# Split first up products, residual plus bias from PSUM, and a split last group in a spectral block with a squared-ReLU feed-forward

## The chip, the cores and the metric

The kernel runs on one core of one Trainium2 chip. The metric is device time in microseconds (us), the median of several executions. One execution was also taken by the hardware profiler; all times inside the kernel come from that one and count from the start of its span.

The engines are called as the profile calls them: PE is the matrix engine and PEld its weight load, DVE the vector engine, ACT the scalar engine, POOL the general engine (idle in the part treated here), SP the engine that issues DMAs. PSUM is the memory with eight banks into which PE writes its products.

## The reference

```python
def _A_ref(x, w_r, w_i):                       # spectral filter
    X = rfft2(x.astype(float32), axes=(-2, -1))
    X = X * (w_r + 1j * w_i)
    return irfft2(X, s=(2048, 512), axes=(-2, -1)).astype(bfloat16)

def _B_ref(x, w1, b1, w2, b2):                 # feed-forward, squared ReLU
    h = einsum("bsd,df->bsf", x, w1) + b1
    r = where(h > 0, h, 0)
    return einsum("bsf,fd->bsd", r * r, w2) + b2

x  = A_x                                       # 1 x 2048 x 512, bf16
h  = x + _A_ref(_layernorm(x), A_w_r, A_w_i)
h2 = h + _B_ref(_layernorm(h), B_w1, B_b1, B_w2, B_b2)   # F = 1792
```

The input `B_x` is not used. The layer norms have no weights of their own.

## The kernel before

The 2048 rows are laid out as 128 partitions by 16 row groups, g = 0 to 15, so that one group is a tile of 128 rows by 512 columns. The kernel has a spectral part, in which the transforms are matrix products with sine tables, and a feed-forward part. The change is in the feed-forward part and in the last inverse transform that feeds it.

**The order of the work.** Every operation is a task of a planner (`Plan`): an engine or a choice of engines, an assumed duration, what it reads and writes, a priority `prio` (small is early) and, for a buffer, an `alloc` tag with a limited number of copies. The planner simulates the engines with the assumed durations, picks at each step the task that can start first (the smallest `prio` among those that can start within 0.08 us of it), and emits the instructions in that order. Each engine then runs its list strictly in order, so an instruction that waits holds up all that stand behind it on its engine. `order` is a weaker form of `reads`: the task comes behind the named one if both are on one engine, and not before the start of the named one otherwise. `uses` keeps a buffer until the task has run.

**PSUM in this part.** Tag `ph` is one bank, `sg` two, `pp` three, `po` two. When a bank is taken and the planner sees PE without work for over 0.4 us ahead of it, `bank` (L678 to L682) first writes some dummy products into that bank (L681, up to 20), which keep PE from standing still. They wait for the bank like any other product.

**Chunks.** The feed-forward goes over five chunks of groups: `CHUNKS = ((0, 2), (2, 5), (5, 9), (9, 13), (13, 16))`. For chunk c the steps are:

- Inverse transform, last step. Chunk 0: `d5` (L703) gives even and odd halves, two groups times two halves; ACT and DVE copy them to `EO` (L708); `d6` adds in one `sg` bank `py` per group the identity product with x (k = 0, L788) and two transform steps (k = 1 and 2, L790 to L793), so that `py` holds h. Later chunks: `s5` (L726 to L729) into a `pp` bank, `od` (L734, ACT) copies its odd half, `lv1` (L739, two on DVE) forms sums and differences, and then one of two ways: groups in `BY_PE2` go straight to PE, `s6` with eight narrow products and one more (L756, L757); the others get a butterfly on DVE, `spec` (L764) and four `lv2` (L772), and then one wide product (L749). DVE adds x (L777, `hs`).
- Layer norm. Sum of squares on ACT (L665; for group 1 statistics on DVE, L803 and L805), a square root on ACT (L806, L840), a reciprocal and a product on DVE, then the normalised rows `u` (L817, L819; later chunks L851, L853).
- Transposes on PE (L828 for chunk 0, L872 for chunks 1 and 2; by DMA for chunks 3 and 4) and the copies to `UT` (L834, L880).
- In chunk 0, `hs` is copied out of `py` for both groups (L822, ACT or DVE). For every group `hb` = `hs` + b2 is formed on DVE (L780), in float32.
- Up products: 14 column blocks f (`NF`), each four products with the chunk's rows as moving operand (L894), into banks taken in turn from `ph`, `sg`, `sg`; then ReLU with bias on ACT (`relu`, L900) and the square on DVE (`sqr`, L906). One block reads all the rows of `UT`, so it waits for the copies of every group of the chunk.
- Down products: per group 14 products of 512 columns into a `po` bank (L915); DVE adds `hb` (`out_`, L923); SP sends the group to memory (L925).

The tasks of the next chunk's inverse transform and layer norm are placed among the up and down products of the chunk before; `early` and `late` are the priorities that do this.

Of the kernel before, what the change touches and what calls it, by code (L numbers as in the profile page):

```python
# [9 lines left out]
ALU = mybir.AluOpType  # L10
ACT = mybir.ActivationFunctionType
FP32 = mybir.dt.float32
BF16 = mybir.dt.bfloat16
# [127 lines left out]
def kernel(  # L141
# [567 lines left out]
            add(("ACT", "DVE"), (0.37, 0.36), deo, reads=[("pd", g, e)], order=[("EO", g, 1)] * (1 - e),  # L709
                writes=[("EO", g, e)], prio=z + g)  # L710

    BY_PE2 = (2, 3, 4, 5, 6)
    ONE = (1, 2, 3, 4)
    TURN = (3, 4)

    for c, (a, b) in enumerate(CHUNKS):
        n = b - a
# [2 lines left out]
        for g in range(a, b):  # L720
            z = late + g
            if c > 0:
                def s5(g=g):
                    p = bank(("p5", g), "pp", 3)
                    lh = [flat(T2[:, lt, g]) for lt in range(4)]
                    mm(p[:, 257:384], lhsT=lh[3], rhs=GI[:, 3, 127:0:-1], start=True, stop=True)  # L726
                    mm(p[:, 384:512], lhsT=lh[2], rhs=GI[:, 2, 128:0:-1], start=True, stop=True)
                    mm(p[:, 0:129], lhsT=lh[1], rhs=GI[:, 1, 128::-1], start=True, stop=True)
                    mm(p[:, 129:257], lhsT=lh[0], rhs=GI[:, 0, 127::-1], start=True, stop=True)  # L729
                add("PE", 0.26, s5, reads=["T2", "GI"], order=gate(c, g - a, n), writes=[("p5", g)], prio=early + 5, alloc=("pp", ("p5", g)))  # L730

                def od(g=g):
                    o = buf(ffn, ("od", g), "od", [P, 2, P], FP32, 2)
                    sc.copy(flat(o[:]), T["p5", g][:, 256:512])  # L734
                act(0.37, od, z, reads=[("p5", g)], order=[("sd", 0, 1)] * (c == 1), writes=[("od", g)], alloc=("od", ("od", g)))

                def lv1(g=g, i=0):
                    q = buf(ffn, ("q", g), "qb" if g in BY_PE2 else "q", [P, 2, 2, P], BF16 if g in BY_PE2 else FP32, 2) if i == 0 else T["q", g]
                    ve.tensor_tensor(q[:, i], T["p5", g][:, 0:256].rearrange("p (a c) -> p a c", a=2),  # L739
                                     T["od", g][:, ::-1, :], (ALU.add, ALU.subtract)[i])  # L740
                for i in range(2):
                    dve(0.36, lambda g=g, i=i: lv1(g, i), z, reads=[("p5", g), ("od", g)],
                        order=[("qh", g)] * i + [("n2", 0, 1)] * (c == 1),
                        writes=[("q", g), ("qh", g)] if i == 0 else [("q", g)], alloc=("qb" if g in BY_PE2 else "q", ("q", g)) if i == 0 else None)

                def s6(g=g):
                    p = bank(("p6", g), "pp", 3)
                    if g not in BY_PE2:
                        mm(p[:], lhsT=KI[:, 0], rhs=T["R", g][:], start=True, stop=True)  # L749
                        return  # L750
                    q = T["q", g]
                    for k in range(4):
                        o = p[:, 128 * k + 1:128 * k + 128]
                        for b in range(2):
                            v = q[:, k // 2, b, :0:-1] if k % 2 == 0 else q[:, k // 2, b, 1:]
                            mm(o, lhsT=KI[:, 1 if b == 1 and k in (1, 2) else 0], rhs=v, start=(k == 0 and b == 0), stop=False)  # L756
                    mm(p[:].rearrange("p (a b c) -> p a b c", a=2, b=2)[:, :, ::-1, 0], lhsT=KI[:, 0], rhs=q[:, :, :, 0],  # L757
                       start=False, stop=True)
                if g in BY_PE2:
                    add("PE", 0.5, s6, reads=[("q", g)], writes=[("p6", g)], prio=early + 4, alloc=("pp", ("p6", g)))  # L760
                else:
                    def spec(e, g=g):
                        R = buf(ffn, ("R", g), "R", [P, 512], BF16, 3)
                        COPY[e](R[:].rearrange("p (a b c) -> p a b c", a=2, b=2)[:, :, ::-1, 0], T["q", g][:, :, :, 0])  # L764
                    add(("DVE", "ACT"), (0.2, 0.27), spec, reads=[("q", g)], writes=[("R", g), ("Rh", g)], prio=z,
                        alloc=("R", ("R", g)))

                    def lv2(g=g, k=0):
                        R, q = T["R", g], T["q", g]
                        x, y = q[:, k // 2, 0, 1:], q[:, k // 2, 1, 1:]  # L770
# [5 lines left out]
                    add("PE", 0.22, s6, reads=[("R", g)], writes=[("p6", g)], prio=early + 4, alloc=("pp", ("p6", g)))  # L776
                dve(0.66, lambda g=g: ve.tensor_tensor(hs[:, g, :], T["p6", g][:], xs[:, g, :], ALU.add), z,  # L777
                    reads=[("p6", g)], writes=[("hs", g)])
                act(0.91, lambda g=g: sq_of(hs[:, g, :], g), z, reads=[("hs", g)], writes=[("ss", g)])
            dve(0.62, lambda g=g: ve.tensor_tensor(hb[:, g, :], hs[:, g, :], b2b[:], ALU.add), late + 180 + g,  # L780
                reads=[("hs", g), ("FW", 3)], order=[("ph", c, 4)], writes=[("hb", g)], shared=True)

        if c == 0:
            for g in range(2):
# [29 lines left out]
                def un0(g=g):  # L814
# [4 lines left out]
                        sc.activation(u[:, 0, :], T["py", 0][:], ACT.Identity, scale=rs2[:, 0:1], bias=nr2[:, 0:1])  # L819
                add(("ACT", "DVE")[g], (0.6, 0.7)[g], un0, reads=[("r2", 0, g), ("n2", 0, g)], writes=[("un", g)] + ["una0"] * (1 - g),  # L820
                    order=["una0"] * g, uses=[("py", g), ("u", 0)], prio=-30.0, alloc=None if g else ("u2", ("u", 0)))
                add(("ACT", "DVE"), (0.59, 0.67), lambda e, g=g: COPY[e](hs[:, g, :], T["py", g][:]), prio=-10.0,  # L822
                    reads=[("un", g)], writes=[("hs", g)], uses=[("py", g)])

                def tr0(g=g):
                    p = bank(("pt", 0, g), "po", 2, BF16)
# [5 lines left out]
                def et0(e, g=g):  # L832
                    u = buf(ffn, ("UT", 0), "UT", [P, 4, ND, P], BF16, 2) if g == 0 else T["UT", 0]
                    COPY[e](flat(u[:, g]), T["pt", 0, g][:, 0:D])  # L834
# [50 lines left out]
        for f in range(NF):  # L885
            z = nxt()

            tag = ("ph", "sg", "sg")[seq[1] % 3]
            seq[1] += 1

            def up(c=c, f=f, n=n, tag=tag):
                p = bank(("ph", c, f), tag, 1 if tag == "ph" else 2)
                for d in range(ND):
                    mm(p[:, 0:P * n], lhsT=W1[:, d, bass.ts(f, P)], rhs=T["UT", c][:, 0:n, d, :],  # L894
                       start=(d == 0), stop=(d == ND - 1))
            add("PE", 0.216 * n, up, reads=[("UT", c), ("FW", 0)], writes=[("ph", c, f)], prio=z, alloc=(tag, ("ph", c, f)))

            def relu(c=c, f=f, n=n):
                r = buf(ffn, ("rl", c, f), "rl", [P, 512], BF16, 6)
# [8 lines left out]
                writes=[("act", c, f), ("act", c)], alloc=("act", ("act", c)) if f == 0 else None)  # L908
        for i in range(n):
            g = a + i  # L910
            for k, (f0, f1) in enumerate(((0, 5), (5, 10), (10, NF))):
                def down(c=c, i=i, f0=f0, f1=f1, g=g):
                    p = bank(("po", g), "po", 2) if f0 == 0 else T["po", g]
                    for f in range(f0, f1):
                        mm(p[:], lhsT=T["act", c][:, f, bass.ts(i, P)], rhs=W2[:, f, :], start=(f == 0),  # L915
                           stop=(f == NF - 1))
                add("PE", 0.217 * (f1 - f0), down,
                    reads=[("act", c, f) for f in range(f0, f1)] + [("FW", 1)], order=[("po", g, k - 1)] * (k > 0),
                    writes=[("po", g), ("po", g, k)], uses=[("act", c)], prio=nxt(), alloc=("po", ("po", g)) if k == 0 else None)

            def out_(g=g):
                o = buf(ffn, ("ot", g), "ot", [P, D], BF16, 3)
                ve.tensor_tensor(o[:], T["po", g][:], hb[:, g, :], ALU.add)  # L923
            dve(0.66, out_, nxt(), reads=[("po", g), ("hb", g)], writes=[("ot", g)], alloc=("ot", ("ot", g)))
            add("SP", 0.1, lambda g=g: sy.dma_start(ov[:, g, :], T["ot", g][:]), reads=[("ot", g)], writes=[("out", g)],  # L925
                prio=nxt())
    plan.run()
    pin(tc, nc)


# [1 line left out]
_INS = ['A_x', 'A_w_r', 'A_w_i', 'B_x', 'B_w1', 'B_b1', 'B_w2', 'B_b2']  # L932
# [26 lines left out]
```

## Time and profile before

| | |
|---|---|
| Median of 8 executions | 166.5 us (165.95 to 167.01) |
| The profiled execution: its own time | 166.49 us |
| its span | 164.7 us |
| PE busy | 156.0 us, 95% of the span |
| DVE busy | 120.4 us, 73% |
| ACT busy | 111.3 us, 68% |
| Granted clock of PE | full over the whole span |

The span runs from the first to the last instruction; the difference of 1.79 us to the execution's own time lies around it. Busy time is the sum over an engine's instructions. PE's matmuls are pipelined and their ends modelled: a wide one is listed with 379 ns although the next one starts 0.22 us later, so PE's share says that it is hardly ever without work and not that it is at its peak. The dummy products count as busy.

A line of the groups reads: line of the kernel, engine, operation, tile written from tile read, shape, count, then busy time, mean duration in ns and the idle time just before.

### The profile page before, as it was taken

What the parts mean: (1) busy time and instruction counts of PE and PEld (TensorE: products, weight loads), DVE (VectorE), ACT (ScalarE), POOL (GpSimd) and SP (SyncE); (2) the same over time, 40 slices, a digit from 0 to 9 for tenths busy, and PEclk for the clock granted to TensorE, in tenths of its full rate; (3) what the DMA queues carried; (4) which work ended last, traced back from release to release, by engine and by line L of the source; (5) the groups of instructions that cost most, each with busy time, mean ns of one, the idle gap of its engine ahead of it and who ended that gap; (6) DMA issues with size and microseconds to landing.
All of it is one profiled execution on the core that took longest, in us unless ns stands there. A gap on an engine that the chain in (4) does not pass through costs nothing.

```text
span 164.7 us, 2906 instructions
## 1 busy us (share of the span) xinstructions
PE 156.0 (95%) x1050; PEld 93.0 (56%) x1059; DVE 120.4 (73%) x341; ACT 111.3 (68%) x212; POOL 16.6 (10%) x41
## 2 busy tenths in 40 slices
PE   7999989999979899999999999999999999999990
PEld 3468867676857786575555544444544444465440
DVE  5999866999976796589994599986298972295211
ACT  8987758998886797469893579861289970188000
POOL 8789600000000000000000000000000000000000
PEclk9999999999999999999999999999999999999999
DMA  5958998993000000010001100025200024010010
GB/s 141 318 177 231 203 294 175 411 355 103 0 4 0 0 4 0 0 66 4 0 0 64 36 0 2 0 53 139 66 4 0 0 55 105 32 36 0 0 64 32
DMA packets 19335, 13.06 MB, mean 79 GB/s; under 512 B 8186, under 2 KB 18042, under 8 KB 19322
## 3 DMA queue, kind: packets, MB, share of 16 engines
q1 hardware_dynamic: 19322, 12.88, 27.7%
q8 instruction: 8, 0.13, 0.3%
q14 instruction: 5, 0.04, 0.1%
HBM read 8.92 MB, written 3.01 MB: 72 GB/s over the span
## 4 chain that ended last, share of the span: by engine, by line
PE 79%; DVE 14%; ACT 2%; issue 2%; DVEq 0%; ACTq 0%
PE po L915 29%; PE sg L894 19%; PE ph L894 10%; PE s_fa L360 5%; DVE m L596 4%; DVE Z L606 3%; DVE M L617 2%; DVE M L619 1%; DVE X L582 1%; PE pp L756 1%; PE m_p L236 1%; PE pp L749 1%; PE s_p L498 1%; PE m_p L404 1%; PE m_p L403 1%
## 5 line engine op out<-in xcount | busy, mean ns | idle before, releaser
L915 PE MATMUL po<-W,act 128*128 128x512 bf16 x215 | 49.5, 379 | 0.5
L900 ACT ACTIVATE rl<-sg,b1f 128x512 bf16<-128x512 f32 (+2 forms) x46 | 27.2, 602 | 18.3 <-PE sg L894 17.0
L894 PEld LDWEIGHTS <-W 128*128 128x128 bf16 x280 | 26.5, 98 | 19.6 <-DVE UT L880 0.3
L894 PE MATMUL sg<-UT,W 128*128 128x512 bf16 (+2 forms) x184 | 37.3, 337 | 0.0
L915 PEld LDWEIGHTS <-act 128*128 128x128 bf16 x224 | 21.7, 98 | 24.3
L906 DVE TENSOR_TENSOR act<-rl 128x384 bf16<-128x384 bf16 (+2 forms) x70 | 24.9, 368 | 8.5 <-ACT rl L900 7.8
L923 DVE TENSOR_TENSOR ot<-po,hb 128x512 bf16<-128x512 f32 x16 | 11.1, 691 | 20.2 <-PE po L915 20.0
L894 PE MATMUL ph<-UT,W 128*128 128x384 bf16 (+2 forms) x96 | 20.4, 335 | 0.0
L900 ACT ACTIVATE rl<-ph,b1f 128x384 bf16<-128x384 f32 (+2 forms) x24 | 14.4, 599 | 7.2 <-PE ph L894 6.5
L777 DVE TENSOR_TENSOR hs<-pp,xs 128x512 bf16<-128x512 f32 x14 | 9.7, 690 | 2.1 <-PE pp L749 1.5
L780 DVE TENSOR_TENSOR hb<-hs,b2b 128x512 f32<-128x512 bf16 x16 | 10.8, 684 | 0.0
L665 ACT ACTIVATE junk<-hs,nm 128x512 bf16<-128x512 bf16 x14 | 10.0, 715 | 0.5 <-DVE hs L777 0.4
L853 ACT ACTIVATE u<-hs,nr,rs 128x512 bf16<-128x512 bf16 x10 | 8.0, 810 | 3.3 <-DVE nr L845 3.2
L477 PE MATMUL m_p<-U,EF 128*128 128x512 bf16 (+1 forms) x46 | 9.4, 337 | 0.0
L384 DVE BATCH_NORM_STATS2 st<-xs 128x6 f32<-128x512 bf16 x13 | 8.4, 671 | 0.4 <-DMA xs<-in_A_x_dram 0.4
L360 PE MATMUL s_fa<-fz 128*128 128x512 bf16 x30 | 8.5, 453 | 0.0
L772 DVE TENSOR_TENSOR R<-q 128x127 bf16<-128x127 f32 x36 | 8.3, 286 | 0.0
L575 ACT CAST AB<-m_p 128x1024 bf16<-128x1024 f32 x7 | 7.1, 1017 | 1.7 <-PE m_p L477 1.7
L653 ACT CAST T<-m_p 128x1024 bf16<-128x1024 f32 x7 | 7.1, 1017 | 0.3 <-PE m_p L643 0.3
L643 PE MATMUL m_p<-EI,M 128*128 128x256 bf16 x48 | 6.4, 274 | 1.0 <-DVE M L617 0.9
L498 PEld LDWEIGHTS <-Bt 128*128 128x128 bf16 x64 | 6.1, 98 | 2.0 <-issue 0.8
L739 DVE TENSOR_TENSOR q<-pp,od 128x256 f32<-128x256 f32 x18 | 6.8, 416 | 0.0
(154 smaller groups left out, 226.9 us busy)
## 6 DMA issues: line engine op xcount, KB each, us to landing
W<-in_B_w_dram SPq DMA_DIRECT2D x2, 1792.0 KB, 10.2
out_dram<-ot SPq DMA_DIRECT2D x16, 128.0 KB, 1.8
xs<-in_A_x_dram SPq DMA_DIRECT2D x4, 256.0 KB, 3.7
xs<-in_A_x_dram SPq DMA_DIRECT2D x2, 512.0 KB, 6.8
W<-wx SPq DMA_DIRECT2D x2, 448.0 KB
W<-in_A_w_r_dram SPq DMA_DIRECT2D x1, 512.0 KB, 7.9
W<-in_A_w_i_dram SPq DMA_DIRECT2D x1, 512.0 KB, 5.9
wx<-in_A_w_r_dram SPq DMA_DIRECT2D x1, 448.0 KB
```

The lines of the kernel that those rows point to most:

```text
L360: mm(p[:, 0:512], lhsT=fz[:, 0:P], rhs=fz[:], start=True, stop=True)
L384: ve.bn_stats(st[:], xs[:, g, :])
L477: mm(o.rearrange("p (j i e) -> p j i e", e=2, i=RUN), lhsT=w, rhs=U[:, q, s].rearrange("p (j e i) -> p j i e", e=2, i=RUN), **k)
L665: sc.activation(junk[:], src, ACT.Square, bias=nm1[:, g:g + 1], accum_out=ss2[:, g:g + 1])
L772: ve.tensor_tensor(o, x, y, (ALU.add, ALU.subtract, ALU.subtract, ALU.add)[k])
L777: dve(0.66, lambda g=g: ve.tensor_tensor(hs[:, g, :], T["p6", g][:], xs[:, g, :], ALU.add), z, reads=[("p6", g)], writes=[("hs", g)])
L780: dve(0.62, lambda g=g: ve.tensor_tensor(hb[:, g, :], hs[:, g, :], b2b[:], ALU.add), late + 180 + g, reads=[("hs", g), ("FW", 3)], order=[ ...
L894: mm(p[:, 0:P * n], lhsT=W1[:, d, bass.ts(f, P)], rhs=T["UT", c][:, 0:n, d, :], start=(d == 0), stop=(d == ND - 1))
L900: sc.activation(r[:, 0:P * n], T["ph", c, f][:, 0:P * n], ACT.Relu, bias=b1f[:, f:f + 1], scale=1.0)
L906: ve.tensor_tensor(t[:, f, 0:P * n], r[:, 0:P * n], r[:, 0:P * n], ALU.mult)
L915: mm(p[:], lhsT=T["act", c][:, f, bass.ts(i, P)], rhs=W2[:, f, :], start=(f == 0), stop=(f == NF - 1))
L923: ve.tensor_tensor(o[:], T["po", g][:], hb[:, g, :], ALU.add)
```

## The change

Four things are altered. The code's new constants `HBP`, `OWN` and `SPLIT` are 0, 1 and 2.

1. The first `SPLIT` = 2 up blocks of chunk 0 are issued in two halves: four products over the 128 rows of group 0, which read only `UT0a` (the copy of group 0), then four over group 1, which read `UT0b`. The first halves have a priority 3000 lower than other up products. Block 0 takes the `ph` bank, block 1 a `po` bank (`UPT`), and the turn of `ph`, `sg`, `sg` goes on with an `sg` bank for block 2.
2. For groups 0 and 1 the copy of `py` to `hs` (L822) and the later `hb` = `hs` + b2 are replaced by one DVE instruction that reads `py` and b2 and writes `hb`. It stands behind the `UT` copies of chunk 0.
3. Group 2's `s6` is put behind up block `SPLIT` = 2 of chunk 0, and chunk 1's `lv1` behind `u` of group 1. Chunk 1's `od` is put behind `u` of group 0 instead of the second square root. `BY_PE2` changes from (2, 3, 4, 5, 6) to (2, 3, 4, 8). In `d6` the identity products (k = 0) of both groups come behind all of `d5` and ahead of the other steps.
4. The last group's down products are issued as two column halves of 256, each 14 products into a bank of its own, with an addition of 256 columns and a DMA of its own.

```diff
-    BY_PE2 = (2, 3, 4, 5, 6)
+    BY_PE2 = (2, 3, 4, 8)
...
+    HBP = 0
+    OWN = 1
+    SPLIT = 2
+    UPT = ("ph", "po")
...
-                act(0.37, od, z, reads=[("p5", g)], order=[("sd", 0, 1)] * (c == 1), writes=[("od", g)], alloc=("od", ("od", g)))
+                act(0.37, od, z, reads=[("p5", g)], order=["una0"] * (c == 1), writes=[("od", g)], alloc=("od", ("od", g)))
...
-                        order=[("qh", g)] * i + [("n2", 0, 1)] * (c == 1),
+                        order=[("qh", g)] * i + [("un", 1)] * (c == 1),
...
-                    add("PE", 0.5, s6, reads=[("q", g)], writes=[("p6", g)], prio=early + 4, alloc=("pp", ("p6", g)))
+                    add("PE", 0.5, s6, reads=[("q", g)], order=[("ph", 0, SPLIT)] * (g == 2), writes=[("p6", g)], prio=early + 4, alloc=("pp", ("p6", g)))
...
-            dve(0.62, lambda g=g: ve.tensor_tensor(hb[:, g, :], hs[:, g, :], b2b[:], ALU.add), late + 180 + g,
-                reads=[("hs", g), ("FW", 3)], order=[("ph", c, 4)], writes=[("hb", g)], shared=True)
+            if c:
+                add(("DVE", "POOL")[HBP], (0.62, 1.3)[HBP], lambda g=g: (ve, gp)[HBP].tensor_tensor(hb[:, g, :], hs[:, g, :], b2b[:], ALU.add),
+                    prio=late + 180 + g, reads=[("hs", g), ("FW", 3)], order=[("ph", c, 4)], writes=[("hb", g)])
...
-                        order=[("pd", g, 0)] + [("py", g, j) for j in range(k)], uses=[("py", g)], writes=[("py", g, k)],
-                        prio=-5000.0 + g - (k == 0), alloc=("sg", ("py", g)) if k == 0 else None)
+                        order=[("pd", 1, 0) if k == 0 else ("pd", g, 0)] + [("py", g, j) for j in range(k)], uses=[("py", g)],
+                        writes=[("py", g, k)], prio=-5000.0 + g - 50 * (k == 0), alloc=("sg", ("py", g)) if k == 0 else None)
...
-                add(("ACT", "DVE"), (0.59, 0.67), lambda e, g=g: COPY[e](hs[:, g, :], T["py", g][:]), prio=-10.0,
-                    reads=[("un", g)], writes=[("hs", g)], uses=[("py", g)])
+                dve(0.69, lambda g=g: ve.tensor_tensor(hb[:, g, :], T["py", g][:], b2b[:], ALU.add), -10.0,
+                    reads=[("un", g), ("FW", 3)], order=[("UT", 0)] * OWN, writes=[("hb", g)], uses=[("py", g)])
...
-                    writes=[("UT", 0)] + ["UT0a"] * (1 - g), prio=-30.0, alloc=None if g else ("UT", ("UT", 0)))
+                    writes=[("UT", 0), "UT0b" if g else "UT0a"], prio=-30.0, alloc=None if g else ("UT", ("UT", 0)))
...
+            first = c == 0 and f < SPLIT
+            tag = UPT[f] if first else ("ph", "sg", "sg")[seq[1] % 3]
+            seq[1] += 1 - (first and tag == "po")
...
+                    mm(p[:, P * i0:P * i1], lhsT=W1[:, d, bass.ts(f, P)], rhs=T["UT", c][:, i0:i1, d, :],
                        start=(d == 0), stop=(d == ND - 1))
...
+            if first:
+                for i in range(2):
+                    add("PE", 0.25, lambda up=up, i=i: up(i0=i, i1=i + 1), reads=["UT0b" if i else "UT0a", ("FW", 0)],
+                        order=[("pf", f)] * i, uses=[("ph", c, f)], writes=[("ph", c, f)] if i else [("pf", f)],
+                        prio=z if i else z - 3000, alloc=None if i else (tag, ("ph", c, f)))
...
+            for h in range(2) if g == G - 1 else (None,):
+                cs = slice(0, D) if h is None else slice(256 * h, 256 * h + 256)
...
+                            mm(p[:, cs], lhsT=T["act", c][:, f, bass.ts(i, P)], rhs=W2[:, f, cs], start=(f == 0),
+                               stop=(f == NF - 1))
...
+                    ve.tensor_tensor(o[:, cs], T["po", g, h][:, cs], hb[:, g, cs], ALU.add)
+                dve(0.66 if h is None else 0.42, out_, nxt(), reads=[("po", g, h), ("hb", g)], uses=[("ot", g)],
+                    writes=[("ot", g, h)], alloc=None if h else ("ot", ("ot", g)))
+                add("SP", 0.1, lambda g=g, cs=cs: sy.dma_start(ov[:, g, cs], T["ot", g][:, cs]), reads=[("ot", g, h)],
+                    writes=[("out", g)], uses=[("ot", g)], prio=nxt())
```

More of the change, by code (lines that the diff above doesn't have):

```diff
@@ L774 @@
                         dve(0.25, lambda g=g, k=k: lv2(g, k), z, reads=[("q", g)], order=[("Rh", g)], writes=[("R", g)])
-                    add("PE", 0.22, s6, reads=[("R", g)], writes=[("p6", g)], prio=early + 4, alloc=("pp", ("p6", g)))
+                    add("PE", 0.22, s6, reads=[("R", g)], order=[("ph", 0, SPLIT)] * (g == 2), writes=[("p6", g)], prio=early + 4, alloc=("pp", ("p6", g)))
                 dve(0.66, lambda g=g: ve.tensor_tensor(hs[:, g, :], T["p6", g][:], xs[:, g, :], ALU.add), z,
@@ L886, with up @@
             z = nxt()
[L888 to L892, printed above, removed]
+            first = c == 0 and f < SPLIT
+            tag = UPT[f] if first else ("ph", "sg", "sg")[seq[1] % 3]
+            seq[1] += 1 - (first and tag == "po")
+            def up(c=c, f=f, i0=0, i1=n, tag=tag):
+                p = bank(("ph", c, f), tag, 1 if tag == "ph" else 2) if i0 == 0 else T["ph", c, f]
                 for d in range(ND):
-                    mm(p[:, 0:P * n], lhsT=W1[:, d, bass.ts(f, P)], rhs=T["UT", c][:, 0:n, d, :],
+                    mm(p[:, P * i0:P * i1], lhsT=W1[:, d, bass.ts(f, P)], rhs=T["UT", c][:, i0:i1, d, :],
                        start=(d == 0), stop=(d == ND - 1))
-            add("PE", 0.216 * n, up, reads=[("UT", c), ("FW", 0)], writes=[("ph", c, f)], prio=z, alloc=(tag, ("ph", c, f)))
+            if first:
[3 more added lines that the diff above has]
+                        prio=z if i else z - 3000, alloc=None if i else (tag, ("ph", c, f)))
+            else:
+                add("PE", 0.216 * n, up, reads=[("UT", c), ("FW", 0)], writes=[("ph", c, f)], prio=z, alloc=(tag, ("ph", c, f)))
             def relu(c=c, f=f, n=n):
@@ L910 @@
             g = a + i
[L911 to L926, printed above, removed]
+            for h in range(2) if g == G - 1 else (None,):
+                cs = slice(0, D) if h is None else slice(256 * h, 256 * h + 256)
+                for k, (f0, f1) in enumerate(((0, 5), (5, 10), (10, NF))):
+                    def down(c=c, i=i, f0=f0, f1=f1, g=g, h=h, cs=cs):
+                        p = bank(("po", g, h), "po", 2) if f0 == 0 else T["po", g, h]
+                        for f in range(f0, f1):
+                            mm(p[:, cs], lhsT=T["act", c][:, f, bass.ts(i, P)], rhs=W2[:, f, cs], start=(f == 0),
+                               stop=(f == NF - 1))
+                    add("PE", (0.217 if h is None else 0.11) * (f1 - f0), down,
+                        reads=[("act", c, f) for f in range(f0, f1)] + [("FW", 1)], order=[("po", g, h, k - 1)] * (k > 0),
+                        writes=[("po", g, h), ("po", g, h, k)], uses=[("act", c)], prio=nxt(),
+                        alloc=("po", ("po", g, h)) if k == 0 else None)
+                def out_(g=g, h=h, cs=cs):
+                    o = T["ot", g] if h else buf(ffn, ("ot", g), "ot", [P, D], BF16, 3)
+                    ve.tensor_tensor(o[:, cs], T["po", g, h][:, cs], hb[:, g, cs], ALU.add)
[3 more added lines that the diff above has]
+                    writes=[("out", g)], uses=[("ot", g)], prio=nxt())
```

## The prediction

> **What bounds the kernel now.** I read the page first (which engine), then the windows by chunk (where that engine is without work), then the chain of waits and the timeline around the one place where it is.
>
> ```profile
> PE 156.0 (95%) x1050; PEld 93.0 (56%) x1059; DVE 120.4 (73%) x341; ACT 111.3 (68%) x212; POOL 16.6 (10%) x41
> ...
> PEclk9999999999999999999999999999999999999999
> ```
>
> ```profile
> 49.00:56.11 7.11, 6.00 (x81) 4.90 (x78) 5.16 (x15) 5.33 (x14) 0.00 (x0) 1.00 0.00 0
> 56.11:69.88 13.77, 13.66 (x117) 9.76 (x116) 10.18 (x33) 9.85 (x25) 0.00 (x0) 1.00 0.00 1
> 69.88:91.22 21.34, 21.24 (x149) 12.51 (x151) 16.87 (x53) 15.25 (x35) 0.00 (x0) 1.00 0.08 26
> ```
>
> Columns: length, then busy time of PE, PEld, DVE, ACT, POOL, and the clock. From 56.11 us, where chunk 0's up products begin, PE lacks 0.1 us of work per chunk; DVE and ACT have 3.6 us and more to spare in each. So the time is PE's list from 56.11, plus what delays its start, plus the tail. The 6.00 us of PE before it flatters: the chain shows dummy products (L681) and other engines' work.
>
> ```profile
> 53.22 0.81 DVE u L817
> ...
> 54.03 0.42 DVE UT L834
> 54.46 0.67 DVE qb L739 x2
> 55.13 0.05 issue
> 55.17 0.62 PE pp L681 x8
> 55.80 0.45 PE pp L756 x8
> 56.24 0.01 PE pp L757
> 56.25 0.46 PE ph L894 x4
> ```
>
> ```profile
> 53.59 0.40 PE L828 MATMUL po<-ident,u 128*128 128x128 bf16 x4 [0.43 <-ACT u L819]
> ...
> 53.70 1.08 ACT L822 CAST hs<-sg 128x512 bf16<-128x512 f32 x2
> ...
> 54.03 0.42 DVE L834 COPY UT<-po 128x512 bf16<-128x512 bf16 x1
> ...
> 54.11 0.39 PE L828 MATMUL po<-ident,u 128*128 128x128 bf16 x4
> ...
> 54.65 0.61 ACT L834 COPY UT<-po 128x512 bf16<-128x512 bf16 x1
> ...
> 57.18 0.91 ACT L900 ACTIVATE rl<-sg,b1f 128x256 bf16<-128x256 f32 x2
> ...
> 69.84 0.46 PEld L894 LDWEIGHTS <-W 128*128 128x128 bf16 x4 [0.30 <-DVE UT L880]
> ```
>
> Group 0's `UT` is ready at 54.45, group 1's at 55.26, yet the first up product starts at 56.11: ahead of it in PE's order stands group 2's `s6`, whose bank comes free only after two `lv1` (55.12), with eight dummies written into that bank first. The last line is the next tight place: chunk 1's first up product waits for its `UT`. At the end, after PE:
>
> ```profile
> L923 DVE TENSOR_TENSOR ot<-po,hb 128x512 bf16<-128x512 f32 x16 | 11.1, 691 | 20.2 <-PE po L915 20.0
> ...
> L739 DVE TENSOR_TENSOR qb<-pp,od 128x256 bf16<-128x256 f32 x10 | 3.9, 417 | 0.5 <-ACT od L734 0.5
> ...
> out_dram<-ot SPq DMA_DIRECT2D x16, 128.0 KB, 1.8
> ```
>
> The last L923 runs from 161.03 to 161.72, then its DMA.
>
> **Part 1, the head of chunk 0.** First halves: UT0a is ready at 54.45, PE sees it 0.05 later (as at 69.79 to 69.84), so eight products of 128 columns run from 54.50, in time in which PE now does nothing useful. Their price is that of L756, eight in 0.45: 56 ns each. All 16 narrow ones cost 0.90 where eight of 256 columns cost 0.88 (L894, four in 0.44). Here a rule speaks against the change: the Trainium skill, "TensorE: Matmul & The Clock Gate", section "Back-to-back issue gap", says that a stream of weight load and matmul pairs sustains only about 81 ns per matmul at 128 columns. By it the second halves alone would cost 8 x 25 ns = 0.2 more on the path (the first halves, 8 x 81 = 0.65, would still just fit before UT0b) and the total below would be 0.2 us later. The row is the same shape with a load for every product, so I take the row and keep 0.2 for the range.
>
> Second halves: ACT loses the two casts (1.08 us, 53.70 to 54.78), so UT0b can be copied when the transposes end, 54.11 + 0.39 = 54.50: by ACT until about 55.13, by DVE (0.42) until 54.95. I take ACT. Second halves run 55.18 to 55.63.
>
> Block 2 needs the `sg` bank of `py` 0, block 3 that of `py` 1. Before, the casts freed both by 54.78; now the `hb` instruction on DVE does. It prices like L777, which also adds a PSUM and an SBUF tile, 690 ns. If DVE does both right after the UT0a copy, they end at 55.14 and 55.83, and blocks 2 and 3 start at 55.63 and 56.07 without waiting. If `lv1` goes first or UT0b falls to DVE, it is up to 0.7 later, and PE waits up to 0.4 for block 2.
>
> At 56.11 PE thus has three blocks behind it (1.32) and group 2's `s6` (0.47: 0.45, and 0.02 for L757) still to do; now it has `s6` done and no block. That is 0.85 ahead. From there blocks come at the ReLUs' pace, about 0.43 (two in 0.91 with their overlap), against 0.44 on PE, because a block takes the bank of the block three earlier; ACT still has one `od` (0.36) and squares of 0.9 to place, and `s6` is no longer there early to fill PE. I take 0.2 off: **-0.65**. Ends: -1.1 (PE full from 54.5 on with no `s6` ahead, 56.11 - 54.50 = 1.61 less 0.47) and 0 (the lead is lost again at 69.84).
>
> What is behind `hb` on DVE: two `lv1` of group 2, and so its `s6` and `hs`, about 1.4 us later. That is hidden as long as PE has up blocks, and on ACT the square of group 2 started at 58.43 behind ReLUs although `hs` was done at 56.98. The two old `hb` (0.68 each, at 59.65 and 61.45) are gone from DVE, so for groups 3 and 4 DVE is even. Chunk 1's `UT` hangs on ACT reaching the square roots (64.38 and 65.90) behind the last ReLUs; these move up with PE, and ACT has 1.08 us less, so I let the lead pass through to 69.84. If that cover fails, the whole 0.65 goes.
>
> **Part 2, edits with one answer.** `od` behind `u` of group 0 and `lv1` behind `u` of group 1: it is the trace's order already (52.78 then 53.44; 53.22 then 54.46). Identity products together: PE has no gap there, group 1's `py` ends as before, group 0's one product (0.21) later; `u` of group 0 starts after the second square root in any case (52.58 and 52.78), so up to 0.1, hidden under DVE's `u` of group 1, which ends 0.5 later. Zero; 0.2 if ACT makes UT0a.
>
> **Part 3, `BY_PE2`.** Groups 5 and 6 leave the narrow `s6` (0.47) for the wide one (0.22), group 8 goes the other way: PE saves 0.25 in chunk 1, where it has 0.1 idle. DVE gains one butterfly there, 0.17 + 0.89 = 1.06: 16.87 becomes 17.93 of 21.34. It is hidden while chunk 2's `UT` beats PE; now it is ready at 89.90 and PE is busy with down products until 91.2. **-0.25**; ends -0.3 and +0.9 (rival C).
>
> **Part 4, the tail.** PE: 28 products of 256 columns at 0.11 (L894) are 3.02, as the 14 wide ones now; the loads (98 ns each) stay under 108. The second bank was read by group 14's addition until 158.70, before the second half starts at about 159.5. The last addition falls from 0.69 to 0.42 (L739 row): **-0.27**. One more issue on SP's queue, 0.33, about 1.5 us before the last, holds up nothing. The last transfer has half the bytes. Here the skill's "DMA: Bandwidth & Descriptors", the fit under the heading "Anatomy of one DMA — SWDGE (gpsimd) path", has 2.0 us fixed plus bytes over 436 GB/s: as an estimate 2.30 for 128 KB and 2.15 for 64 KB, so 0.15 more gained. The trace lands 128 KB in 1.8, under that fixed part, on another path; I count 0, with -0.15 to +0.1 (512-byte rows, and the first half still in flight).
>
> **Sum.** -0.65 - 0.25 - 0.27 = -1.17 on the profiled execution's own 166.49 (span 164.7 and 1.79 around it) gives 165.3. The median is 166.5, so the execution stands for it.
>
> **Rivals.**
> - B, the lead is lost at chunk 1. The 0.30 at 69.84 speaks for it: `UT` has no slack there, and group 2's chain starts later. Against it: ReLUs set the square roots. Parts 3 and 4 alone: 166.49 - 0.52 = 166.0.
> - C, slower: DVE is late for chunk 2. Groups 5 and 6 both put a butterfly on the path (2.1 us) before group 8's shorter way helps. The slack of 1.3 shrinks by PE's lead (0.9) to 0.4, so PE stands 1.7 us at chunk 2's first up block: 166.49 - 1.17 + 1.7 = 167.0. It decides from the point where the last `UT` copy of chunk 2 comes over 0.4 us later against the trace's 89.90; it makes the whole slower at 1.6. The 4.5 us that DVE has free in chunk 1, and ACT's 6.1 for copies, speak against it. Half of it gives 166.2.
> - D, the bank waits take part 1: the planner may put dummies ahead of block 2 as it did at 55.17 (eight, 0.42), or `lv1` ahead of `hb`. Part 1 falls to -0.2: 165.8.
> - E, the first halves don't run early, because the planner's UT0a comes on ACT behind two `od`: part 1 is about -0.4, 165.6.
>
> **How the numbers follow.** A median change under 0.3% (0.5 us) can't be told from none here. Main line 0.50 (165.3; its own range 164.8 to 165.7), D and E together 0.20 (165.6 to 165.8), B 0.16 (165.7 to 166.3), C 0.09 (166.2 to 167.0), a larger gain 0.05 (to 164.6). Faster means below 166.0: all of the main line, D, E, the larger gain, and a third of B: 0.80. Same, 166.0 to 167.0: two thirds of B and half of C: 0.15. Slower: 0.05. The range 164.7 to 166.2 leaves out most of C, a little of B and the largest gains.
>
> **What would show it.** Right: eight L894 products of 128 columns near 54.5; no L681 in a `pp` bank at 55.2; the cast lines gone, two additions from `sg` of 0.69; three blocks done near 56.1; chunk 1's first up block near 69.2 and chunk 2's near 90.3, with no PEld idle over 0.3 before either; the last addition 0.42, starting about 0.9 earlier. Wrong: chunk 1's first block still near 69.8 (B), PEld idle of 1 us before chunk 2's (C), or narrow products spaced by 80 ns.

## The result, and the profile after

| | before | changed |
|---|---|---|
| Median | 166.46 us (32 runs, 165.95 to 167.06) | 165.33 us (11 runs, 165.07 to 165.83) |
| Ratio | | 0.9931, 95% interval 0.9918 to 0.9944 |
| The profiled execution, its span | 166.49, 164.7 us | 165.09, 163.3 us |

The kernel became 1.13 us faster by the medians; 1.17 was predicted, as 165.3. The profiled executions differ by 1.40, of which 0.19 lies ahead of anything that was changed: the first `d6` product starts at 50.13 before and at 49.94 after. So stages are counted from that product below. The end of the span, counted in this way, comes at 114.58 before and at 113.34 after, 1.24 earlier.

The changed kernel's page and its windows, cut at the first up product of chunk 0, 1 and 2 (length, then busy time of PE, PEld, DVE, ACT and POOL, then the clock):

```profile
PE 155.1 (95%) x1052; PEld 93.5 (57%) x1061; DVE 121.3 (74%) x346; ACT 110.9 (68%) x211; POOL 16.9 (10%) x41
...
PEclk9999999999999999999999999999999999999998
```

```profile
49.00:54.38 5.38, 4.82 (x57) 3.61 (x54) 4.14 (x13) 3.52 (x11) 0.00 (x0) 1.00 0.00 0
54.38:68.84 14.46, 14.35 (x130) 10.43 (x132) 10.78 (x35) 11.19 (x28) 0.00 (x0) 1.00 0.03 10
68.84:89.92 21.08, 20.97 (x141) 12.14 (x142) 18.10 (x58) 15.17 (x35) 0.00 (x0) 1.00 0.06 20
```

PE still lacks 0.1 us of work per chunk. Chunk 0's stage starts 1.73 earlier (54.38 against 56.11) but is 0.69 longer: group 2's `s6` (0.47) is now inside it, PE stands 0.15 between the first and the second halves until it sees group 1's copy, and block 3 waits 0.06 for its bank. Chunk 1's stage is 0.26 shorter with 1.23 more DVE work in it. The chain of waits shows the head (L839 copies `UT`, L900 is the up product, L760 and L761 are `s6`):

```profile
53.90 0.44 DVE UT L839
...
54.38 0.38 PE ph L900 x4
54.76 0.22 PE po L900 x4
54.99 0.37 PE ph L900 x4
55.35 0.22 PE po L900 x4
55.58 0.93 PE sg L900 x8
56.50 0.45 PE pp L760 x8
56.95 0.01 PE pp L761
```

The two lines "PE po L900 x4" are block 1's halves: 0.22 for four products of 128 columns with four weight loads. The first halves run before group 1's copy is done, blocks 0 to 3 all stand ahead of `s6`, and no dummies stand ahead of `s6`. The timeline around it:

```profile
54.33 0.59 ACT L839 COPY UT<-po 128x512 bf16<-128x512 bf16 x1 [0.38 <-PE po L833]
...
54.57 1.28 DVE L827 TENSOR_TENSOR hb<-sg,b2b 128x512 f32<-128x512 f32 x2
...
56.34 0.61 PE L760 MATMUL pp<-qb,KI 128*128 128x127 bf16 x8
...
68.62 0.64 PEld L900 LDWEIGHTS <-W 128*128 128x128 bf16 x4
```

ACT reaches group 1's copy 0.38 before it can start; DVE adds b2 to the h of both groups from `sg` in 1.28, and block 3 (the second half of the `sg` line at 55.58) starts at 55.91, right behind their end at 55.85; the weight load of chunk 1's first up product waits for nothing, where PEld had stood 0.30. At chunk 2 the last `UT` copy is only just in time:

```profile
89.26 0.59 ACT L885 COPY UT<-pp 128x512 bf16<-128x512 bf16 x1 [1.14 <-PE pp L877]
...
89.92 1.03 PE L900 MATMUL ph<-UT,W 128*128 128x512 bf16 x4
```

The copy ends at 89.85 and PE starts at 89.92, straight behind its down products. Before, 1.3 lay between the two. The tail, in the chain and in the DMA issues:

```profile
159.77 0.42 DVE ot L938
```

```profile
out_dram<-ot SPq DMA_DIRECT2D x15, 128.0 KB, 1.8
out_dram<-ot SPq DMA_DIRECT2D x2, 64.0 KB, 1.5
```

### The profile page after: what moved, and what is told of

Read it like the earlier page. It is cut to its first block, busy times and chain, and to the rows that moved or that the text cites. A ratio compares the mean times of both kernels' runs of the same rounds, so it can differ in the third digit from the quotient of the medians.

```text
span 163.3 us, 2919 instructions
## 1 busy us (share of the span) xinstructions
PE 155.1 (95%) x1052; PEld 93.5 (57%) x1061; DVE 121.3 (74%) x346; ACT 110.9 (68%) x211; POOL 16.9 (10%) x41
## 4 chain that ended last, share of the span: by engine, by line
PE 73%; DVE 13%; ACT 5%; DMA 4%; issue 2%; SPq 1%; DVEq 0%; ACTq 0%
PE po L929 29%; PE sg L900 20%; PE ph L900 10%; DVE m L596 4%; DMA xs<-in_A_x_dram 4%; DVE Z L606 3%; DVE M L617 2%; DVE M L619 1%; DVE X L582 1%; PE pp L753 1%; PE s_p L498 1%; ACT Bt L419 1%; PE pp L760 1%; SPq L265 1%; ACT junk L378 1%
## 5 line engine op out<-in xcount | busy, mean ns | idle before, releaser
L929 PE MATMUL po<-W,act 128*128 128x512 bf16 (+1 forms) x229 | 49.7, 366 | 0.5
L912 ACT ACTIVATE rl<-sg,b1f 128x384 bf16<-128x384 f32 (+2 forms) x46 | 27.4, 603 | 18.1 <-PE sg L900 16.9
L900 PEld LDWEIGHTS <-W 128*128 128x128 bf16 x288 | 26.8, 98 | 19.6 <-issue 0.2
L900 PE MATMUL sg<-UT,W 128*128 128x384 bf16 (+2 forms) x184 | 37.5, 337 | 0.0
L929 PEld LDWEIGHTS <-act 128*128 128x128 bf16 x238 | 23.0, 98 | 22.9
L938 DVE TENSOR_TENSOR ot<-po,hb 128x512 bf16<-128x512 f32 (+1 forms) x17 | 11.2, 660 | 19.5 <-PE po L929 19.3
L900 PE MATMUL ph<-UT,W 128*128 128x512 bf16 (+3 forms) x96 | 19.9, 330 | 0.1
L912 ACT ACTIVATE rl<-ph,b1f 128x512 bf16<-128x512 f32 (+2 forms) x23 | 13.9, 603 | 3.6 <-PE ph L900 2.8
L665 ACT ACTIVATE junk<-hs,nm 128x512 bf16<-128x512 bf16 x14 | 10.0, 714 | 1.2 <-DVE hs L781 1.1
L776 DVE TENSOR_TENSOR R<-q 128x127 bf16<-128x127 f32 x40 | 9.5, 285 | 0.0
L785 DVE TENSOR_TENSOR hb<-hs,b2b 128x512 f32<-128x512 bf16 x14 | 9.5, 682 | 0.0
L477 PE MATMUL m_p<-U,EF 128*128 128x512 bf16 (+1 forms) x46 | 9.4, 337 | 0.0
L743 DVE TENSOR_TENSOR q<-pp,od 128x256 f32<-128x256 f32 x20 | 7.7, 416 | 0.0
```

What stands on the lines that cost most here:

```text
L477: mm(o.rearrange("p (j i e) -> p j i e", e=2, i=RUN), lhsT=w, rhs=U[:, q, s].rearrange("p (j e i) -> p j i e", e=2, i=RUN), **k)
L665: sc.activation(junk[:], src, ACT.Square, bias=nm1[:, g:g + 1], accum_out=ss2[:, g:g + 1])
L785: add(("DVE", "POOL")[HBP], (0.62, 1.3)[HBP], lambda g=g: (ve, gp)[HBP].tensor_tensor(hb[:, g, :], hs[:, g, :], b2b[:], ALU.add), prio=lat ...
L900: mm(p[:, P * i0:P * i1], lhsT=W1[:, d, bass.ts(f, P)], rhs=T["UT", c][:, i0:i1, d, :], start=(d == 0), stop=(d == ND - 1))
L912: sc.activation(r[:, 0:P * n], T["ph", c, f][:, 0:P * n], ACT.Relu, bias=b1f[:, f:f + 1], scale=1.0)
L929: mm(p[:, cs], lhsT=T["act", c][:, f, bass.ts(i, P)], rhs=W2[:, f, cs], start=(f == 0), stop=(f == NF - 1))
```

## The experiments

From each profile five starts are taken: the first `d6` product, the first up product of chunk 0, 1 and 2, and the last addition. Four stages lie between them (us). They repeat to 0.02 where nothing was changed, whereas whole executions of one kernel spread over 0.8 and more. Each ratio is to the kernel before in the same session, whose median was 166.46, 166.54, 166.58 or 166.63, so compare ratios and not medians between the rows.

| kernel | `d6` to chunk 0 | to chunk 1 | to chunk 2 | to last addition | median | ratio to before, interval |
|---|---|---|---|---|---|---|
| before | 5.98 | 13.77 | 21.34 | 69.81 | 166.46 | |
| changed | 4.44 | 14.46 | 21.08 | 69.85 | 165.33 | 0.9931 (0.9918 to 0.9944) |
| e1 whole blocks | 5.02 | 15.08 | 21.08 | 69.85 | 166.51 | 1.0 (0.9986 to 1.0013) |
| e3 casts | 4.43 | 15.16 | 21.09 | 69.84 | 165.97 | 0.9968 (0.9955 to 0.9981) |
| e7 `s6` order only | 5.18 | 14.64 | 21.34 | 69.81 | 166.49 | 1.0001 (0.9988 to 1.0014) |
| e9 no dummies | 5.53 | 13.77 | 21.34 | 69.81 | 166.14 | 0.9972 (0.9961 to 0.9983) |
| e4 tail whole | 4.44 | 14.45 | 21.09 | 69.81 | 165.27 | 0.9924 (0.9909 to 0.994) |
| e5 old paths | 4.44 | 14.45 | 21.35 | 69.84 | 165.52 | 0.9934 (0.9919 to 0.995) |
| e6 tail, one DMA | 4.43 | 14.46 | 21.09 | 69.84 | 165.21 | 0.9913 (0.9895 to 0.9931) |
| e8 cut at 384 | 4.44 | 14.46 | 21.08 | 69.85 | 165.14 | 0.9913 (0.9896 to 0.9929) |
| e10 same plan, whole | 5.03 | 14.24 | 21.09 | | 165.62 | 0.9944 (0.9927 to 0.9961) |
| e12 old orders | 4.81 | 14.78 | 21.09 | | 166.21 | 0.9978 (0.9968 to 0.9988) |
| e13 old `d6` order | 4.54 | 15.16 | 21.08 | | 166.01 | 0.9963 (0.9952 to 0.9974) |
| e11 casts, no dummies | 4.44 | 14.82 | 21.09 | | 165.93 | 0.9954 (0.9936 to 0.9972) |

### The kernel before with one edit

**e9: the dummies ahead of group 2's `s6` left out.**

```diff
-                    p = bank(("p6", g), "pp", 3)          # may write dummies first
+                    p = bank(("p6", g), "pp", 3, dry=g == 2)   # bank writes none for group 2
```

> The kernel before with one edit: no dummy products are written into group 2's s6 bank ahead of s6. My theory: s6 starts at 55.17 instead of 55.63 and all of PE's list behind it comes 0.45 earlier, 166.0, as far as chunk 1's UT also comes earlier. Rival: chunk 1's first up block is held by its UT at 69.8 whatever PE does before; then nothing is gained, 166.4, and PEld idles about 0.7 before that block.

The chain of waits of this kernel:

```profile
54.23 0.67 DVE qb L739 x2
54.91 0.05 issue
54.95 0.62 PE pp L756 x8
55.58 0.46 PE ph L894 x4
```

Chunk 0 starts 0.45 earlier, the stage behind it is as long as before, and the ratio agrees (0.28% of 166.5 is 0.47). The eight dummies are the only difference in the weight loads up to chunk 1. Nothing at chunk 1 held the lead back, so my theory holds: 0.45, against 0.85 that the whole change earned up to chunk 1, was to be had by not writing dummies into a bank that comes free late. They do not fill a gap there: before, the dummies start at 55.17, 0.05 after the second `lv1`; here `s6` starts 0.05 after it. They waited for the same release as the product behind them.

**e7: group 2's `s6` behind up block 2.**

```diff
-    add("PE", 0.5, s6, reads=[("q", g)], writes=[("p6", g)], ...
+    add("PE", 0.5, s6, reads=[("q", g)], order=[("ph", 0, 2)] * (g == 2), writes=[("p6", g)], ...
```

> The kernel before with one edit: group 2's s6 stands behind up block 2 of chunk 0. My theory: the first block starts when group 1's UT is seen, 55.3 instead of 56.1, but s6 (0.47) still has to be done, so only the eight dummies of 0.42 and some of the wait are saved: about 0.35 us faster than before, 166.1. Rival: the place of s6 and its dummies was the whole cost; then this one edit gains about 0.8, 165.65, and the split of the blocks adds little.

Both were wrong: no gain. The chain of waits:

```profile
54.16 0.97 ACT hs L822 x2
55.13 0.50 ACT UT L834
...
55.67 0.60 PE ph L894 x4
56.27 0.87 PE sg L894 x8
57.14 0.45 PE pp L756 x8
...
59.40 0.39 PE pp L681 x7
59.79 0.45 PE pp L756 x8
```

Chunk 0 starts 0.80 earlier, as the theory had it (when group 1's copy, here behind both casts on ACT, is seen), and its stage grows by 0.87: `s6` (0.47), which has only moved, and seven dummies (0.39) that the planner now puts ahead of another group's `s6`. So the old dummies are gone and others have come. What the move gains without the new ones was not run; by these numbers it is an estimated 0.33. In the changed kernel the same order is without effect: the planner gives every engine the same list without it.

### The changed kernel with one part undone

**e1 and e10: blocks 0 and 1 issued whole.** e1 leaves the planner to plan anew. e10 keeps its plan: the first-half task only takes the bank, and the second emits the whole block.

```diff
-            if first:                    # e1
+            if False:
```

```diff
+                if first:                # e10, in up()
+                    if i0 == 0:
+                        return
+                    i0 = 0
```

> The changed kernel, but up blocks 0 and 1 of chunk 0 are issued whole (four products of 256 columns each, in the same ph and po banks); all else as changed. My theory: the first halves earn what they do because they run while PE waits for group 1's UT. Whole, both blocks start at about 54.97 and end at 55.85 instead of 55.41, so everything behind is 0.4 us later: chunk 1's first up block about 0.4 later against the start of the first d6 product, time about 165.7. Rival: the ReLUs' pace sets the blocks from number 3 on, or the gain came from moving group 2's s6; then the two halves are worth at most 0.15 and the time stays at 165.3 to 165.5.

> The changed kernel with the same order of instructions on every engine; only the eight narrow first-half products of blocks 0 and 1 are not issued early, and the blocks are issued whole where their second halves stood. My theory: this is the worth of the split alone. The blocks run 0.88 us from group 1's UT on instead of 0.45, so chunk 1's first up block comes 0.4 later (19.3 after the first d6 product instead of 18.9) and the time is 165.7. The 1.2 us that the kernel with whole blocks lost in the first study is then mostly the planner's other order. Rival: the split alone is worth the whole 1.2, and this kernel takes 166.5; or PE has slack before chunk 1 and it loses nothing.

In e10 the chain of waits is that of the changed kernel with the blocks behind group 1's copy:

```profile
54.49 0.59 ACT UT L839
...
55.12 0.60 PE ph L904 x4
55.72 0.44 PE po L904 x4
56.16 0.87 PE sg L904 x8
```

Chunk 1's first up product comes 5.03 + 14.24 = 19.27 after `d6`, against 18.90: the split is worth 0.37. That is the 0.44 of eight narrow products less the 0.06 that block 3 now waits for its bank. e1 lost 1.20 there. Its start is the same as e10's, so the other 0.84 lies between chunk 0 and chunk 1, where its chain shows the new plan:

```profile
68.47 0.45 PE pp L877 x8
68.91 0.86 PE po L929 x4
69.77 0.24 PE pp L877 x4
...
70.03 0.59 ACT UT L885
...
70.67 0.48 PE sg L900 x2
```

Chunk 1's last transpose comes behind the down products, ACT copies it while PE has nothing but dummies for 0.66, and only then can chunk 1 begin. The theory holds for the split, and the large loss of e1 is mostly that of another plan.

With e7 and e10 the 0.85 up to chunk 1 can be put together. Moving `s6` brings 0.80 less its own 0.47, that is 0.33 (e7, without its new dummies). Chunk 0 then starts at 5.18 in e7 and at 5.03 in e10, where group 1's copy no longer stands behind the casts: 0.15. The split brings 0.37. No dummies come back in e10: its stage of 14.24 is the old 13.77 and `s6`.

**e3 and e11: casts and late `hb` put back.** e11 also leaves out the dummies ahead of chunk 0's up blocks.

```diff
-            if c:
+            if True:                     # hb for groups 0 and 1 as well
...
-                dve(0.69, lambda g=g: ve.tensor_tensor(hb[:, g, :], T["py", g][:], b2b[:], ALU.add), -10.0, ...
+                add(("ACT", "DVE"), (0.59, 0.67), lambda e, g=g: COPY[e](hs[:, g, :], T["py", g][:]), prio=-10.0, ...
```

> The changed kernel, but with the copies of py to hs and the later hb = hs + b2 for groups 0 and 1 put back as before; all else as changed. My theory: with a cast on ACT group 1's UT copy comes up to 0.3 later, and the two hb of 0.68 are again on DVE among the squares; the banks come free earlier, but blocks 2 and 3 don't wait for them in the changed kernel. Net 0.2 to 0.5 us slower than the changed kernel, about 165.6. Rival: the casts fit between ACT's other work, DVE has 3.6 us to spare, and the time is that of the changed kernel within 0.1.

> The kernel with the casts put back, but with no dummy products ahead of any up block of chunk 0. With the casts chunk 1's first block came 0.69 later than in the changed kernel, and six dummies (0.49) stood ahead of an up block at 58.6, with a wait of 0.19 before them. My theory: the dummies are most of that loss, so 0.4 to 0.5 comes back and the time is about 165.5: the residual from PSUM itself is worth 0.2. Rival: PE was waiting for ACT there in any case, the dummies only filled the wait, and the time stays at 165.9 to 166.0.

e3's chain of waits:

```profile
57.41 0.82 ACT junk L665 x2
58.22 0.37 ACT rl L912
...
58.63 0.49 PE sg L681 x6
59.13 0.44 PE sg L900 x4
```

ACT does a square (L665) ahead of a ReLU, the ReLU frees a bank late, PE waits for it and then writes six dummies into it before the up block. (The piece is listed with 0.49; from the first dummy to the up product it is 0.33.) In e11 the profile gives 0.34 back (14.82 instead of 15.16) and keeps 0.36, almost all of it the wait: in both kernels the up product or dummy at this place starts 0.46 after the product ahead of it, where 0.11 is the usual distance. The times cannot tell e3 and e11 apart (the intervals overlap). By the stages the residual from PSUM is worth 0.36 without the dummies and 0.69 with them. I had expected 0.2, and for another reason: group 1's copy is hardly late (the second halves start 5.10 after `d6` instead of 5.03), the cost came later, in ACT's order.

**e12 and e13: the small orders put back**, which the prediction had at zero.

```diff
-    order=["una0"] * (c == 1)            # e12, od
+    order=[("sd", 0, 1)] * (c == 1)
...
-    [("un", 1)] * (c == 1)               # e12, lv1
+    [("n2", 0, 1)] * (c == 1)
```

```diff
-    order=[("pd", 1, 0) if k == 0 else ("pd", g, 0)] ...  prio=-5000.0 + g - 50 * (k == 0)   # e13
+    order=[("pd", g, 0)] ...                              prio=-5000.0 + g - (k == 0)
```

> The changed kernel with two weak orders put back: chunk 1's od behind the second square root and lv1 behind the product n2 of group 1, as before. In the prediction I put these at zero. In this plan one lv1 of group 2 stands ahead of u of group 1 on DVE, and two more ahead of group 0's UT copy. My theory now: the first up products come 0.4 plus 0.75 us later, so most of the head's gain goes, and the time is 166.1 to 166.4. Rival, the prediction's: the orders are worth nothing, 165.3.

> The changed kernel with the identity products of d6 in their old places. In the prediction I put this at zero, because PE has no gap there. The planner's lists differ here too: u of group 0 is put in earlier, and od and lv1 follow another order. My theory: the d6 products themselves cost nothing either way, but the plan that follows does, 0.2 to 0.6 slower than the changed kernel. Rival, the prediction's: zero, 165.3.

e12, chain of waits:

```profile
52.89 0.35 ACT od L738
53.24 0.69 ACT u L824
...
59.36 0.39 PE pp L681 x7
```

`od` now runs ahead of `u` of group 0 and chunk 0 starts 0.37 later; seven dummies follow. Together 0.69 are lost by the stages, and 0.9978 against 0.9931 agrees with that (0.78). e13, chain of waits:

```profile
53.55 0.54 ACT od L738 x2
54.08 0.55 ACT UT L839
...
68.93 0.24 PE pp L877 x4
...
69.19 0.59 ACT UT L885
...
69.83 0.81 PE sg L900 x4
```

Two `od` stand ahead of group 0's copy, now on ACT, so chunk 0 starts 0.10 later; and chunk 1's last transpose is planned behind down products, as in e1, so that PE has nothing but dummies for 0.66 before chunk 1. Together 0.80 by the stages; the ratios give 0.53, and their intervals do not rule 0.80 out.

The 0.69 and the 0.80 must not be added. The planner works from the kernel's text alone, so its lists can be had without a run. The kernel before, with nothing changed but the place of the identity products, already gets `od` ahead of `u` of group 0 and an `lv1` ahead of `u` of group 1. And with the identity products in their old places the two small orders change no list: e13 without them is the same kernel. So the new `d6` order makes the planner put `od` and `lv1` in early, and the small orders forbid it. By the stages the new `d6` order alone is then worth 0.10 (19.69 in e13 to 19.59 in e12, from `d6` to chunk 1; the ratios, 0.9963 and 0.9978, do not show it), and the small orders on top of it 0.69.

**e5: `BY_PE2` as before.**

```diff
-    BY_PE2 = (2, 3, 4, 8)
+    BY_PE2 = (2, 3, 4, 5, 6)
```

> The changed kernel with BY_PE2 as before, (2, 3, 4, 5, 6). My theory: PE has 0.25 us more work in chunk 1 and nothing else changes, so chunk 2's first up block is 0.25 later against chunk 1's, and the time is 165.6. Rival: DVE's extra butterfly in the changed kernel costs something that is got back here; then the time is the same or lower, and chunk 2's first up block not later.

Chunk 1's stage is 21.35 instead of 21.08, 0.27, about what the two kinds of `s6` differ by (0.25 expected). The ratio, 0.9934 against 0.9931, is too coarse to see it.

**e4, e6, e8: the tail.** e4 has the last group whole, e6 sends both halves in one DMA, e8 cuts at 384 columns.

```diff
-            for h in range(2) if g == G - 1 else (None,):                                      # e4
+            for h in (None,):
```

```diff
+                if h == 0:                                                                     # e6
+                    continue
-                ... sy.dma_start(ov[:, g, cs], T["ot", g][:, cs]), reads=[("ot", g, h)]
+                ... sy.dma_start(ov[:, g, :], T["ot", g][:]), reads=[("ot", g, h)] + [("ot", g, 0)] * (h == 1)
```

```diff
-                cs = ... slice(256 * h, 256 * h + 256)                                         # e8
+                cs = ... (slice(0, 384), slice(384, D))[h]
```

> The changed kernel, but the last group's down products, addition and DMA are whole as before. My theory: 0.27 us slower than the changed kernel (the last addition 0.69 instead of 0.42; PE's 28 products take what the 14 take; the landing is the same), 165.6. Rival: the narrow products cost PE something or the smaller transfer lands no sooner and the end of the program takes longer; then the difference is about 0.1, as the spans of the two profiles suggest (from PE's last product to the end of the span 3.67 before, 3.53 changed).

> The changed kernel, but the last group's two halves are sent by one DMA of 128 KB after the second addition. My theory of the tail: the addition alone earns 0.27, the size of the last transfer nothing, so the time is that of the changed kernel, 165.3. Rival: the 64 KB landed in 1.5 us where 128 KB takes 1.8, so one DMA is 0.3 slower, 165.6, and half of the tail's gain is the transfer's.

> The changed kernel, but the last group's columns are cut at 384 instead of 256, so that the last part has 128 columns. My theory: the last addition falls from 0.42 to about 0.28 (128 columns of float32 at the slope of 0.27 per 256), the 14 products of 128 columns cost 56 ns each as in L756, so 0.1 to 0.15 us faster than the changed kernel, 165.2. Rival: weight loads of 98 ns are no longer hidden under products of 56 ns in a row of 14, which costs up to 0.6, or 256-byte rows land more slowly; then 165.4 to 165.9.

Counted from each kernel's first `d6` product (us):

| | last addition starts | last DMA issue | end of the span | issue to end |
|---|---|---|---|---|
| changed, two DMAs of 64 KB | 109.83 | 110.28 | 113.34 | 3.06 |
| e4, whole | 109.79 | 110.51 | 113.45 | 2.94 |
| e6, one DMA of 128 KB | 109.83 | 110.28 | 113.22 | 2.94 |
| e8, cut at 384 | 109.82 | 110.14 | 113.10 | 2.96 |

The shorter addition brings the last issue forward by 0.23 (0.27 less 0.04 on PE), but the end comes only 0.11 earlier, which is e4's rival and not its theory. The smaller transfer does land sooner (1.5 us against 1.8), yet from the issue to the end it is 0.12 longer. The waits of SP show where, first in the changed kernel, then in e4:

```profile
SPq L969 <- PEq L969: 0.6, 2, 0.4
```

```profile
SPq L969 <- PEq L969: 0.2, 1, 0.2
```

After the last landing SP goes through a closing sequence. In the kernels with two DMAs for the last group it waits 0.4 more in it, which the profile puts down to PE's sequencer. In those with one DMA it does not. Why is open. e6 keeps the short addition, has one DMA, and ends 0.12 before the changed kernel. In e8 the 14 products of 128 columns start 56 ns apart, with a new weight load for each, so they cost PE nothing more; the shorter addition and the earlier landing bring its end 0.24 forward. These are single profiles, and none of it can be told apart by the ratios (0.9931, 0.9924, 0.9913 and 0.9913), whose intervals overlap.

## Why the prediction was right, and where it was not

**The head of chunk 0: -0.65 predicted, -0.85 measured** (18.90 instead of 19.75 from `d6` to chunk 1). The mechanism is the predicted one, with a lead passed on in full to chunk 1. The mis-sized term is the 0.2 that I took off for the ReLUs' pace: 0.85 had been worked out without it, and the profile shows no wait of PE for a ReLU in this stage. Group 1's copy on ACT (54.33), and the narrow products at 55 ns, were as put down. The rule of 81 ns per product, cited in the prediction, was not seen, neither in this stage nor for the 14 products in a row of e8. Of rival D one `lv1` did stand ahead of the two additions, at a cost of 0.06 for block 3; no dummies came. Rival E is what e13 shows, `od` twice ahead of group 0's copy on ACT, at a cost of 0.10 at the start.

**What the 0.85 is made of was not seen.** The prediction had the dummies as one circumstance among others; by themselves they are 0.45 (e9). The split is 0.37 in the plan that was chosen (e10). The losses of the other experiments do not add up like that: each of these edits, undone alone, costs more than its own work, because the planner answers with another order (e1, e12, e13).

**"Edits with one answer": zero predicted; 0.80 lost with all of them undone (e13), 0.69 of it by the two small orders alone (e12).** This is the step that failed. I argued that the trace already had these orders. It had them in the old plan. In the new one it would not have them by itself: e12's lists have `od` ahead of `u` of group 0 on ACT and one `lv1` ahead of `u` of group 1 on DVE. It is the new order of `d6` that brings this about, by the planner's lists. Part 1 came out nearly right because it was worked out with the old order of those instructions, which is what the small orders keep. What I charged as zero was a condition of part 1.

**`BY_PE2`: -0.25 predicted, -0.26 measured**, and e5 has it alone at 0.27. DVE in chunk 1 rose to 18.10 of 21.08 us (17.93 of 21.34 expected), chunk 2 was not late, so rival C did not occur. It was close: the last `UT` copy ended 0.07 before the first up product, where the prediction still counted on 0.4. But ACT had waited 1.14 for the transposes, so PE's own order set that copy, and not DVE. Rival B did not either: chunk 1's first weight load waits for nothing.

**The tail: -0.27 predicted, -0.11 measured** (end of the span, against e4). The last addition is 0.42 as priced and the last issue moves by 0.23. The prediction counted 0 for the transfer, between -0.15 and +0.1; from the issue to the end it became 0.12 longer, a little outside.

**Sum.** Up to the last issue the profiles give 0.85 + 0.26 + 0.23 = 1.34; the longer closing takes 0.1 back, and the spans from `d6` on differ by 1.24. The medians differ by 1.13, with an interval of about 0.2 either way. The predicted 1.17 had the head 0.20 too small and the tail 0.16 too large. That the two errors nearly cancel is luck.

## What to carry to other kernels

Count for a saturated engine two things: what is in its list, and where it stands without work. An item that is only moved within the list costs its own time again at the new place (`s6` in e7). Taking out filler that waits for the same bank as the work behind it gained all of its time (0.45, e9), and running half an item in a gap gained nearly all of it (0.37 of 0.44, e10). With a planner that reorders by assumed times, an edit that only fixes an order can look free in the old trace and be what holds the new plan together, so undo it in the new plan before calling it free. And read the tail to the end of the span: the last issue moved by 0.23, the end by 0.11.

## What was not expected of the hardware

The first `d6` product started anywhere from 49.90 to 50.57 us in these profiles, though no instruction ahead of it differs. This spread is nearly as large as that of whole executions (165.07 to 165.83 for the changed kernel), while every stage behind it repeats to 0.02. From the first product of L477, in the spectral part, to the first `d6` product it is 28.43 to 28.45 in every profile, so the spread arises earlier, in the first 22 us. So that early part, not the part studied, limits what the times can tell. Its cause was not tried.

The last transfer's landing fell from 1.8 to 1.5 us with half the bytes, and the end of the span came later after the issue and not sooner (3.06 against 2.94): with two DMAs SP waits 0.4 more in its closing sequence. The cause of that wait stays open.
